# Another order of the same blocks: new tables for a hand-ordered attention and SwiGLU kernel

## The chip, the cores and the metric

The kernel runs on one core of one Trainium2 chip. A core has TensorE (matmuls, with weight loads shown on a row of their own), VectorE (DVE), ScalarE (ACT), GpSimd (POOL) and SyncE (SP), which here issues nearly all DMAs. Each engine works through its own instructions strictly in the order in which they were written, and waits where an input or a buffer is not ready. The metric is the device time of one execution in microseconds.

## The reference

For each of four batches, 32 inducing points attend to 12416 rows of x, which gives a small matrix h; then every row of x attends to h. The result goes through an RMS norm and a SwiGLU block with 1536 hidden columns, in FP32.

```python
def mab(q, kv):
    s = scale * (q @ kv.transpose(0, 2, 1))
    s = s - s.max(-1, keepdims=True)
    a = np.exp(s)
    a /= a.sum(-1, keepdims=True) + 1e-09
    return a @ kv
h = mab(I, x)                         # (4, 32, 128)
x = mab(x, h).reshape(B * S, D)       # (49664, 128)
...
rms = np.sqrt(np.mean(x * x, axis=-1, keepdims=True) + 1e-06)
xn = x / rms * rms_g
g = xn @ w_gate
silu = g * (1.0 / (1.0 + np.exp(-g)))
val = xn @ w_val
return (silu * val @ w_out).astype(np.float32)
```

## The kernel before

**Units and blocks.** A batch is cut into seven sets of rows (five of 2048, one of 1920, one of 256), and the first six sets into four quarters: 25 units of 512, 480 or 256 tokens each, 100 units over the batches. For each unit the twelve slices of 128 hidden columns are worked through one by one. A unit and a slice make a block; there are 1200.

**What a block does.** The second attention's weights, normalised so that the RMS norm is already in them, stand in a tile `a` as two rounded halves (`hi`, `lo`, each 32 rows, twice). The products of h with the gate and value weights stand as halves in `sg` and `sv`. So a gate is one matmul in the fast FP32 format, `gate` (L709), and a value one more, `value` (L737). ACT takes SiLU of the gate (`silu`, L719), DVE multiplies with the value (`times_value`, L751) and gives u. Then u is projected by the output weights `wo`, in one of three ways, the block's kind:

- P: `project_plain`, one plain FP32 matmul of u (L807, input `u,wo`).
- S: the product stays in PSUM; ACT makes a high half (L764), DVE the low half (L770), two matmuls project them (L795, L796) into one accumulator, POOL adds the halves in place (L815), and a third matmul projects the sum (L807, other inputs) into the other accumulator.
- D: as S, but u goes to SBUF, ACT makes the high half (L761), POOL the low one (L777), ACT scales the high one down (L783), and from the two matmuls on it is like S.

When a unit's blocks are done, `scale_up` (ACT, L839), `finish` (DVE, L848) and `turn_out` (DVE, L854) make its output, which `store` writes with four DMAs (L867). `gather` brings a unit's `a` together with four DMAs from the halves (L647); two such tiles are in turn.

**What runs beside.** While the blocks of one batch run, the attention of the next is prepared in small steps: loads of x by channels (`load_channels`, L111), DVE transposes of them (L299), scores (L316), exponentials, sums (L369), the output weights' halves, the norm (L548 to L608) and the split into halves (L627 to L635). There are 871 such steps, `micros`. At the start, weights are rounded on DVE, ACT and POOL (L204 to L260) and multiplied with h (`stack_of`, L485).

**What sets the order.** Nothing is scheduled when the kernel is built. One long string, `program`, is read letter by letter: `g` is a gate, `s` a SiLU, `v` a value, `m` the product, `h`, `l`, `n`, `e` the halves, `q` the two projection matmuls, `d` the addition, `r` the third matmul, `p` the plain projection, `E F T O` the end of a unit, `a` a gather, and a dot is the next of the `micros`, whose numbers stand in `taken`. Every engine gets its share of this sequence in this order. Further tables say which buffer each step takes: `banks` which of the eight PSUM banks, `holders` which of the nineteen tiles for u and its halves, `workers` and `outputs` which work and output tile; `sorts` gives the kind of each block, and `picks` which of the waiting blocks a letter takes. The loop that reads them (`do` maps letters to steps):

```python
for name in "".join(program.split()):
    made = len(nc.cur_bb.bb.instructions)
    step, args = micros[int(next(taken))] if name == "." else (do[name], ())
    step(*args)
```

Waits follow from data and buffers: a step that writes a bank or tile waits for the last reader of what stood in it.

Of the kernel before, what the change touches and what calls it, by code (L numbers as in the profile page):

```python
# [23 lines left out]
def kernel(  # L24
# [12 lines left out]
    m = inducing.shape[0]  # L37
# [1144 lines left out]
    def seams():  # L1182
# [13 lines left out]
        0234567021437052637152613076123067216073126071362016720162071620761270627410741203741231502137502137502153701530  # L1196
        7513074136507431570431672541765726152641756401725672543712453743143524750137502367261732107301627012670430123727
        2457321741357436527365202760327325036725032746326047312630140172403274015274312453714714671356717354107235410245
        1324135042130531073506735031756305617051253720372430520374053745236074537630431031706473061372461267514742764521
        7426543172632516730257156701350357064317064306247604062475027064571427015701537414213547231472513467541350463150  # L1200
        4135046530241564363016430176301746301724630716207516205321056310261405631574316371536741670456306751067102652057
        2570126507142571245714235174271354270643276345276527346275327464152364526345324502643056413206415027561207561057
        6120376253172142674561426541270564217045720437142741037126407236257342653475367264157637164314017360713604137607
        4153756345315215634160254310523104571230451204750416205421602364013503052413547032451724657142637162314761234712
        3467123061421325614532426756053075620562357230167501653176417534675671362457214235120321370157312510367250617564
        6246041712160421736230173616071561637601563075643764532645234256325143521463251305402503254234720472536420736027
        3464167462061270416071521050616521063215031025463152603176031635071736051630154702432124157134512745163721641206
        4236143613260413670326470260237052670325710263517253237543154713273561247623407636270612071023610256751467251462
        5176514725641357613615617036710536057167102571271470254724107521460152403514325431423014250145301504305450370457
        6302456730245632431206523026312560712037614261013071437201357240153425304614620136014620132014327345207354037540  # L1210
        2354673046215406215046510265402650264765072673250632753604327453715052054517420714756210425601352103210650263501
        7653145075065351375061750537215403140537120142307203142031643127532654512435625142305364502347052367327642576324
        7321437250437524375240732605413251427141346124361724173062413602410536140351406351436547065203405306524502340267
        3402640230634026413062167403641036401351463514056734256741265243124631623562041354163257435731516547635016741571
        2056215625460216452130420643274320436076204753264357614213471362376423016720472014564152420641205340263275602475
        2760574025176254637251372457143152307451204715276510761026517365023640576042734350423754210753702132370210726135
        2071362073462130143061402134561042615067156215427546172534526134063456145601634507645174607462071274126702671347
        0360135017673617536072361251725374327341534752362145362341301503520450137243031702310612067032613760521705620412
        7405170124073517354014607436746574053764052364721307063710726317503274052374062032764271603274026703653627620756
        735062731567235627  # L1220
    """
    workers = """
        2012012012012011021021120120120102201211210210201022012021021021
    """
    outputs = """
        10101010101010101010101010101010101010101010101010101010101010101010101010101010101010101010101010101010
    """
    holders = """
        abcdefghiabdcejkflmgnohibapqdrscefhgljibmkedpqnorscalhgfbmjiednkcgorfabdpsieqlmocgnpafrshkjdbqlimonregqlcspmoakj
        fhdqlbspnimrqkolesjgpncmraqdohfkiblsmpnojrqkmelnspgcjqaromsblhdfkpnjroicqmlgasnerkbplojqmfsdrhqnkaplmogbsrikjpql  # L1230
        ncmofesrkjdhpmlnaqogbcisrdkjlnepmhqkjolnpmfjosabrlnpcmjdoqgkhrlnpsoemjikrlnfqpbcsmjoldaqkspnmrjlqgoknhesicprfmlo
        qjnkspdormbgjeknqpslomjqrhaksonpfirlmjcqdobnrekpmshjqgloanikfrjpmslqndokrsbjlcpmeqohgnkraifpmsjbcelqhondgkrsjpml
        oqnikfcbpralsemjhgdoqcbkpenrlmsjfgoqkpalmisjnorkdqplmbhcnroqklefgsmpjaknilrdohqsbcmefpgadicjkafnliropqbsmjkcdnrp
        lfoqghasmeijkbncrpdfglohiqsjmebakngqsrpfjmdchiloegknfqsbrpkcajnqlsodrmpkqgiljhnsapbcdermokqnsplhaojkrqfgsnlmojkr
        dpqiblmcsnekroajslngmphqkorfdljcnqbkmspliornjqkemlsporangqhdfieskjmbciopaqldrnjmshrfnjqslgcbaokeprnqimljsdonkqph
        fcrmlobkqgnjaspedrmfhncigbjlokqsrmepnjlqsrmpnqodkscrmjlbqhokaspniefqrgmjlospkqdnclbosmhkanroqmpejsglkfonqrmlipch
        jsdoknqrmpjlboksrmnlapoegsqkjmrlposkqjmfnrlpoihkjcbaqlsmepndokgrjfsqhomrljkcpnisqoramljbekpsnfdqogrmhjlkpscqaieb
        jkglrpofsncqmhijkaedpoblsgrncqjfhmkpiabrnelmpgfqsjkordplmnqjahombckpnsirqefjlgkdpnahsormbckqejplnrsigfdkojqampcr
        lbesnhjqfkmiopdrlsnajqckmoprgbejlhsniqrokpmjsfdlacqneprmjgoshlbifcqnkmpjrodslagkqnmipjsherlckoqpfjnbmsrdkgaljqok
        pinmecrsfljhakpgqbinodcmrslqkjneposfalqhmkbgrjdcenspmokifrjalpqmohbnlgersipjkqomnfrcbpsdjkglohqmrnjpkeloasqbmrnj  # L1240
        pgcfklosinjmqahrpdecbgikladmqnofijrhbcspgklmqaednfoklspjrmnohqklpbicsjrqknmlorkpnsqgjmefoklrnpqhjdoabslikmcqjfrn
        pokqmgsjlrponmkqsjlrpondkslbhjmerpqnikasloqcnkjfghesldrnpomkqjsbcalpmokhqrsnjlikpemqdrfgcosnbkjamoilphqredgsnfbk
        jclpmoqrsnakjilpmoqrhsedfmnlobkpgcajqrslomnikphfloersdmnjqckprlsmojgbnqaifkpojhsrlmedcgnqsobaifhkjedglmcrpsnqklo
        bjmfrpeqsaknildgcjmoqhsknlbrfapoiqjrmskneplcoqjdrmskgnphljofqrbmsaknplojiqrcmeskodpjnmgblqfsrokpjnhsrmolkapqnjsi
        emroldkpqscnjoblkmpfrqhsnjompgerlkjoaqmspirndkljocbfhqmspkelgirnqmspajlkdohrcbfqnsjmoprgkeqlsnijmaporkqfslcbpnoj
        rmkshqdlrogmeijpqkclnsrabomfjpqhdiklgsnjqrpomsekncjlrabopfmqskdjhlonrgpmskqlijoncbprmskqeljnofpramsdkgqlhpicbenj
        mroskpqflmrosknjdpqhrgosaklmnpicqjbokesrflmpqnhsjdlraopmqkngscoljbmipksoqnedlrjmasoqfhpnkjmgcsloqprmnbiedkjsplra
        monkfqgjslprmcoqhnkjeslbipramnkoqjdgsfhlmpkocqnjrislaemopqjhnrdksbplfjmngkcioqsrpnljmkaeoshdqlfgrpicjnbae
    """
    sorts = """  # L1250
        PPPPPPPPPPPPPDDDPPPSPDPPDPPDPDPSSDPPDPDPPDPPPPPSDDDPDPDPSPSPSDPDSSPPPPSSPSSSSDSPSDPSSPDSSSSSSSDPSPSDDPSSPSPSDPSD
        SSDSSSSSPSDSPSSPPSSPSPDDPPDPSPSSPSDSSSDSPSDPSSPSSSPSDSSPPSDSPSSSSSSDPSSPDSSSSSSSPSSSSSSSSDSDPSSSSDPSSPSPSSSSSSSP
        PSDDDSPPSSPDPPSPPSDSSSSPDPSPDPDPSDPPSSPSPSSPDSSSPSPPSSPSPPSPSSPSPDSDPDPPPDPPSSDPSSDDDPDPPPSSDPDPSPPSPPSPSDDDPPPS
        PDPSPSDSSDSSSPDDPDPSSSSSPSSDSSSDDPPSPSSSSDPSSPSDPPSSSSSSDSSPSSSDPSPDPDSPSSSSSSSSDPSSSPSPSSSDDPSDPDPPSPPPSDSSSDSS
        SSSDPSSPSSDPSPDSSSSPSSSSSSSSDPSPSSDSPPSSSSSSSSSSSSSSSSSSDSSSPPDPSDSPSPDPSSSSPSPSSDSDPSPDSSPSSSSDSPSDPDPPPSPDSDPS
        PPSPDSDPSSSSPSSPPSDPSSPPPSSPSPPSSPPSSDSSDPSDDPSDPSPPSSDSPSSPSPSPSPSDSSDPSPSPSDDPPDSSSSDPPSSPSDSDSPPSSSDSSDDPSPPD
        SPSPPDSSSSPSDDDPPPDSSDPSPSSSDSPSSSSSDPSDSPSSSSDSSPSSDPSDDPPSPPSPSDPDDPPSPDPPSPSSSSSSDSPSSSSSSSSSPSDSSSSDSPSPSPSS
        SSSSSSSSSSSSDDSSPSSDSSPSDSSSSPPSSSSSSDSDPSSPPSDSDPDPPSPPPSSSSSDSPSSPPDSSPDPPSSSDDPSPSPSSPSSSPSPPPPSSSDPPPPSSDDPP
        PSPSDSSSDPSPDDPPSSDSSPPSSPSSSSSPSSSSPSPSSPSSDSPSSPSSSSPDSPSSSSSSPSSSDSSPSSPSSSSDPSSPPSSSSSDSDSPSPSSSPSSSDSSSPSPS
        SSSDSPSSPSSSDPSSSSPSSSSPSSDDPSPSSSSPSSSSSDSSPPSSSPSSSDSSPSSPSSSDSDPSPSSPSSSPSSSSSSSSDPSSPSSDSPSPSPSSSDSPSSSPSSSS  # L1260
        SSDPSPSSPSSSSDSSSPSPSSDSSPSSSSPSDSPDSPSSSSPSSSSSSPDPSSSPSSPDSSPSSSSSPSPDPDPDPPPP
    """
    picks = """
# [231 lines left out]
```

## Time and profile before

| | |
|---|---|
| median of three runs | 1481.76 us (1481.65 to 1482.52) |
| profiled execution | 1481.53 us |
| its span in the trace | 1479.7 us |
| granted TensorE clock | 0.999 |
| first gate product at | 47 us |
| DMA queue of SyncE | 114.55 MB, 39.8% of 16 engines' span |

The profile gives, for each engine, the time in which it is busy; records of neighbouring instructions overlap, so a sum over instructions exceeds the busy time. A row of a group shows the line in the kernel, the engine, the operation, what it writes and reads, the count, the busy time, the mean length of one in ns, and then how long the engine was idle just before such an instruction and what ended that.

### The profile page before, as it was taken

What the parts mean: (1) busy time and instruction counts of PE and PEld (TensorE: products, weight loads), DVE (VectorE), ACT (ScalarE), POOL (GpSimd) and SP (SyncE); (2) the same over time, 40 slices, a digit from 0 to 9 for tenths busy, and PEclk for the clock granted to TensorE, in tenths of its full rate; (3) what the DMA queues carried; (4) which work ended last, traced back from release to release, by engine and by line L of the source; (5) the groups of instructions that cost most, each with busy time, mean ns of one, the idle gap of its engine ahead of it and who ended that gap; (6) DMA issues with size and microseconds to landing.
All of it is one profiled execution on the core that took longest, in us unless ns stands there. A gap on an engine that the chain in (4) does not pass through costs nothing.

```text
span 1479.7 us, 26001 instructions
## 1 busy us (share of the span) xinstructions
PE 1467.6 (99%) x7286; PEld 1102.4 (74%) x7286; DVE 1420.0 (96%) x2469; ACT 1309.5 (88%) x2605; POOL 1378.8 (93%) x1204
## 2 busy tenths in 40 slices
PE   9999999999999999999999999999999999999998
PEld 6566777877777777787777777777778777787787
DVE  6999998999999999999999999899999999999997
ACT  5798889889988898988998988988998989899997
POOL 1499998999999999999999999999989999999998
PEclk9999999999999999999999999999999999999999
DMA  7694324448453231465656321264232122222122
GB/s 286 129 127 94 68 40 92 88 116 128 78 102 73 42 70 32 94 136 103 116 89 117 56 44 29 43 136 107 58 63 45 33 38 38 42 38 42 36 43 35
DMA packets 391712, 116.28 MB, mean 79 GB/s; under 512 B 365584, under 2 KB 370704, under 8 KB 389008
## 3 DMA queue, kind: packets, MB, share of 16 engines
q1 hardware_dynamic: 390976, 114.55, 39.8%
q8 instruction: 58, 0.95, 0.3%
q14 instruction: 86, 0.70, 0.2%
q10 hardware_dynamic: 592, 0.08, 0.0%
HBM read 53.95 MB, written 27.00 MB: 55 GB/s over the span
## 4 chain that ended last, share of the span: by engine, by line
PE 94%; DVE 2%; DMA 1%; issue 1%; ACT 1%; POOL 0%; SPq 0%; DVEq 0%; ACTq 0%; POOLq 0%
PE gv L807 31%; PE gv L709 17%; PE gv L737 17%; PE gv L795 12%; PE gv L796 12%; PE gv L316 3%; PE gv L369 1%; PE gv L908 1%; DMA xn<-in_x_dram 1%; DVE u L751 0%; PE gv L569 0%; DMA xT<-in_x_dram 0%; PE gv L463 0%; DVE o L239 0%; DVE we L248 0%
## 5 line engine op out<-in xcount | busy, mean ns | idle before, releaser
L719 ACT ACTIVATE silu<-gv 128x512 f32<-128x512 f32 (+2 forms) x1200 | 671.4, 592 | 74.4 <-PE gv L709 55.9
L815 POOL TENSOR_TENSOR xn<-xn,xn 128x512 fp32r<-128x512 f32 (+2 forms) x486 | 605.0, 1264 | 15.5 <-PE gv L796 14.0
L709 PE MATMUL gv<-a,sg 128*128 128x512 f32 (+2 forms) x1188 | 482.1, 431 | 0.6 <-DMA a<-lo 0.6
L737 PE MATMUL gv<-a,sv 128*128 128x512 f32 (+2 forms) x1188 | 449.4, 411 | 0.3 <-ACT silu L719 0.2
L751 DVE TENSOR_TENSOR gv<-silu,gv 128x512 f32<-128x512 f32 (+2 forms) x643 | 422.1, 676 | 10.2 <-PE gv L737 5.0
L764 ACT ACTIVATE xn<-gv 128x512 fp32r<-128x512 f32 (+1 forms) x629 | 370.0, 598 | 32.9 <-DVE gv L751 27.0
L751 DVE TENSOR_TENSOR u<-silu,gv 128x512 f32<-128x512 f32 (+2 forms) x557 | 354.5, 652 | 12.2 <-PE gv L737 5.3
L807 PE MATMUL gv<-u,wo 128*128 128x512 f32 (+2 forms) x724 | 353.5, 573 | 1.1 <-DVE u L751 1.0
L770 DVE SCALAR_TENSOR_TENSOR xn<-xn,gv 128x512 fp32r<-128x512 f32 (+1 forms) x516 | 337.4, 664 | 8.9 <-ACT xn L764 6.2
L709 PEld LDWEIGHTS gv<-a,sg 128*128 128x128 f32 x1188 | 223.3, 189 | 106.6 <-issue 32.4
L737 PEld LDWEIGHTS gv<-a,sv 128*128 128x128 f32 x1188 | 222.9, 189 | 86.9 <-issue 21.4
L815 POOL TENSOR_TENSOR xn<-xn 128x512 fp32r<-128x512 f32 (+1 forms) x204 | 255.3, 1257 | 7.0 <-PE gv L796 4.0
L777 POOL TENSOR_TENSOR xn<-u,xn 128x512 fp32r<-128x512 f32 (+2 forms) x174 | 218.2, 1260 | 15.7 <-ACT xn L761 15.2
L815 POOL TENSOR_TENSOR u<-xn,u 128x512 fp32r<-128x512 f32 (+2 forms) x133 | 167.9, 1271 | 2.1 <-PE gv L796 1.9
L795 PE MATMUL gv<-xn,xn 128*128 128x512 f32 (+1 forms) x441 | 169.7, 385 | 0.0
L807 PEld LDWEIGHTS gv<-u,wo 128*128 128x128 f32 x724 | 134.9, 190 | 27.9 <-issue 10.9
L795 PE MATMUL gv<-xn,more 128*128 128x512 f32 (+2 forms) x355 | 137.6, 388 | 0.0
L796 PE MATMUL gv<-xn,xn 128*128 128x512 f32 (+2 forms) x363 | 135.9, 374 | 0.0
L807 PE MATMUL gv<-xn,xn 128*128 128x512 f32 (+2 forms) x363 | 135.0, 383 | 0.5 <-POOL xn L815 0.3
L783 ACT ACTIVATE xn<-xn 128x512 fp32r<-128x512 f32 (+2 forms) x194 | 122.0, 633 | 10.8 <-POOL xn L777 9.2
L761 ACT ACTIVATE xn<-u 128x512 fp32r<-128x512 f32 (+2 forms) x194 | 121.0, 625 | 6.9 <-DVE u L751 6.1
L807 PE MATMUL gv<-xn,more 128*128 128x512 f32 (+2 forms) x311 | 118.8, 396 | 0.0
(223 smaller groups left out, 1787.8 us busy)
## 6 DMA issues: line engine op xcount, KB each, us to landing
out_dram<-o SPq DMA_DIRECT2D x320, 64.0 KB, 2.0
xT<-in_x_dram SPq DMA_DIRECT2D x60, 256.0 KB, 4.6
xn<-in_x_dram SPq DMA_DIRECT2D x60, 256.0 KB, 5.8
a<-hi SPq DMA_DIRECT2D x156, 64.0 KB, 2.0
a<-lo SPq DMA_DIRECT2D x156, 64.0 KB, 2.0
xn<-in_x_dram SPq DMA_DIRECT2D x5, 1024.0 KB, 9.6
xn<-w SPq DMA_DIRECT2D x18, 256.0 KB, 4.2
out_dram<-o SPq DMA_DIRECT2D x64, 60.0 KB, 2.0
```

The lines of the kernel that those rows point to most:

```text
L709: nc.tensor.matmul(g[:, 0:T], stacks[b][0][:, ts(j, P)], halves_in_turn(one["a"][:, 0:T]), start=True, stop=True)
L719: nc.scalar.activation(sl[:, 0:T], gates.pop(n)[:, 0:T], AF.Silu)
L737: nc.tensor.matmul(v[:, 0:T], stacks[b][1][:, ts(j, P)], halves_in_turn(one["a"][:, 0:T]), start=True, stop=True)
L751: nc.vector.tensor_tensor(out=to, in0=sl[:, 0:T], in1=v[:, 0:T], op=ALU.mult)
L764: nc.scalar.activation(hi, t["u"], AF.Copy, scale=-(1.0 - 2.0 ** -13) * 2.0 ** -12)
L770: nc.vector.scalar_tensor_tensor(out=t["lo"], in0=t["hi"].bitcast(F32), scalar=4096.0, in1=t["u"], op0=ALU.mult, op1=ALU.add)
L777: nc.gpsimd.tensor_tensor(out=t["lo"], in0=t["u"], in1=t["hi"].bitcast(F32), op=ALU.subtract)
L783: nc.scalar.activation(t["hi"], t["hi"].bitcast(F32), AF.Copy, scale=-(2.0 ** -12))
L795: nc.tensor.matmul(to, weight_of(0, j), halves_in_turn(t["hi"]), start=not one["q"], stop=False)
L796: nc.tensor.matmul(to, weight_of(1, j), halves_in_turn(t["lo"]), start=False, stop=last)
L807: nc.tensor.matmul(to.rearrange("p (n h) -> p h n", h=2) if step2 else to, lhsT, rhs, start=one["left"] == NJ, stop=one["left"] == 1)
L815: nc.gpsimd.tensor_tensor(out=t["lo"], in0=t["hi"].bitcast(F32), in1=t["lo"].bitcast(F32), op=ALU.add)
```

## The change

The eight tables `program`, `taken`, `banks`, `outputs`, `holders`, `workers`, `sorts` and `picks` have new contents; no function and no buffer changes, and neither does anything ahead of the first gate on TensorE. (`workers` and `outputs` are short, with 64 and 104 entries as before.) The new `program` has 10920 letters instead of 10915; `taken` names the same 871 steps in another order, most of it close to the old one. In `sorts`, P stands 358 times instead of 362, S 658 instead of 643 and D 184 instead of 195.

```diff
     banks = """
-        0234567021437052637152613076123067216073126071362016720162071620761270627410741203741231502137502137502153701530
+        0234567023147502635270132567123657315627316275312675321753215327512571632571624503125301543254132501543015430543
...
     workers = """
-        2012012012012011021021120120120102201211210210201022012021021021
+        2102102102102201021021210210210202102112120120102011022121021021
...
     sorts = """
-        PPPPPPPPPPPPPDDDPPPSPDPPDPPDPDPSSDPPDPDPPDPPPPPSDDDPDPDPSPSPSDPDSSPPPPSSPSSSSDSPSDPSSPDSSSSSSSDPSPSDDPSSPSPSDPSD
+        PPPPPPPPPPPPPPPPSPDPDPSPDDDPPPSPSPSPPDPDPPSDPPPSDDPDPDDPPPSPPSPSSSPSDPSSPPDSSDPSSPSSPDDSSDSPDPSSPPSSSDSSSSSDSSPS
...
     taken = """
-        9 1 0 5 10 80 6 2 7 54 41 81 13 3 45 106 108 46 4 11 17 55 42 18 47 43 107 19 25 12 21 26 14 56 29 20 15 105 59
+        1 0 5 54 9 80 2 6 79 41 3 10 81 4 42 17 13 7 18 106 43 107 11 25 12 19 45 108 21 55 20 46 44 8 26 14 56 105 22
...
```

The beginnings of the two sequences, dots with their numbers, show the kind of change (first gates, SiLUs, values, products and plain projections):

```
before  9 1 0 g 5 g 10 80 6 s s 2 g 7 g 54 41 s g 81 v v v 13 3 45 106 m 108 m 46 p s m 4 s g 11 v s
after   1 0 5 g g 54 g 9 80 s 2 s 6 79 g s 41 3 10 g 81 v v v m v 4 42 17 s 13 7 18 p 106 m 43 107 m s v p m
```

More of the change, by code (lines that the diff above doesn't have):

```diff
@@ L1200 @@
[L1200 to L1204, printed above, removed]
@@ new lines @@
+        5430571467051042014627461047614270642703460265346035631345104165340637416345617456724561451724650721543725305230
+        5132735012360123642106346013602143620135624015360213021703612031027126410745070725741704215704621740624061720710
+        4172307230647236472347524763257463250631740137503704157345713014356143643565136416325146320513605235062307253620
+        7305136576351764516375134761547316423172037601630172361023512571047303451353457031560457625472504256406247064256
+        7305436304653416534165034153642052030632705635726703156273162743526352143615243160540367543175107154031754013407
@@ new lines @@
+        1342716041304043716041426374263543564736247357436734504165304606143651307461354647316413672416471364120764231453
+        1736724172347631026124360456413651326342516325136216731247121342731207340731271540724072450762450642705642063726
+        5316310321352126017235013623564561263264135246175326715265237067526352760327560256123546256146315236540236401267
+        4320174031403127405214305230154025604125607421065465215326152364156241531120615205160526572160527165230572347120
+        3712347013402374235730576037526035706325602743262160240321401642132405640627060265742062750641706247601763026127
@@ new lines @@
+        6320513705610354131603416035401263402343641730643107634136075416034670142704327034130247104352102641345342164524
+        3716534653416540361543615403726107316053610736501765370614315764274314515612346152015304102410254725107425170517
+        4021174621637217427614302673407542762735230560536720562071025704251254123053150145213602436130121420134723140237
+        0254120417264127412754163542715267546257620674250725463072540372150720342017240723127602375253672032635273052617
+        0527156261264724572164731524713547307031274012734016273465706102170272467410673216425102510235610526130235067026
@@ new lines @@
+        SPSSDSPPSSSSSSSSDPSSDSPPSSSDSSPSSSSSPSSDSSDSDSPPSSPSSPSSSSSPPSSDDSDPPPPSPPSSDPSPSDPPSSSSSSSSSSSSSSSSSSPDPSSSPDPS
+        SSSSSSPSSDSSSSSSSSDSSDPSDSPSPDSPSPSSSSSSSSPDSDSDSPSPPPSPPSSSPSDDPSSPSPDPDPDPDPSPPSSPSSSDPSPSSSPPPSPSPSSPSSSDDPSP
+        SSPSDPDPDDSSPSSPSSPSSSSDPPSPPPSSSSSSSSSPSDSDSPSSPSSPSSSSSSSSDSPSPSSSSSSDSPPPSSSSSPSPDSPSSSSSSSDPSPSSSSSDSPSSSSDS
+        PPSSSSSDSPPSSSSSSDPSSPPSSSSSSSSSPSSPSDSDSPSSPSSPSDSSSSPDSPSSPSSSSDSPSSPSSSSSSDPSSPSPSSSSSSSSDSPSSSPSSSDDSPPSPPSS
+        SSSDPSSPSSPSSSSSSSPSSDSSPSSSDSPPSSSSSSSDPSSPPSSDSSSPSSPSSPSSDSSPSSSPSSSPSDPDPPPP
```

367 lines of the change are left out of this document (176 added, 191 removed), and 58 rows, old and new, of the table taken.

## The prediction

> **What bounds the kernel.** I read the page first: the busy shares, then the chain that ended last.
>
> ```profile
> span 1479.7 us, 26001 instructions
> ...
> PE 1467.6 (99%) x7286; PEld 1102.4 (74%) x7286; DVE 1420.0 (96%) x2469; ACT 1309.5 (88%) x2605; POOL 1378.8 (93%) x1204
> ...
> PE 94%; DVE 2%; DMA 1%; issue 1%; ACT 1%; POOL 0%; SPq 0%; DVEq 0%; ACTq 0%; POOLq 0%
> ```
>
> Four engines are nearly full, and the chain of waits is TensorE. Its busy share alone does not prove that it streams at its rate, because the records of successive matmuls overlap. So I looked at start times in its timeline (start, duration, both in us):
>
> ```profile
> 1000.02 1.02 PE L807 MATMUL gv<-u,wo 128*128 128x512 f32 x2
> 1000.48 0.78 PE L709 MATMUL gv<-a,sg 128*128 128x512 f32 x1
> 1001.10 0.38 PE L795 MATMUL gv<-xn,xn 128*128 128x512 f32 x1
> 1001.31 0.38 PE L796 MATMUL gv<-xn,xn 128*128 128x512 f32 x1
> 1001.53 0.38 PE L709 MATMUL gv<-a,sg 128*128 128x512 f32 x1
> ```
>
> Matmuls of 512 columns start 0.216 us apart (1001.10, 1001.31, 1001.53). I call that a pass. The plain FP32 projection (kind P, two records) and the gate behind it take 1001.10 - 1000.02 = 1.08 us, that is, five passes: four for P, one for the gate. Kinds S and D project with three passes (L795, L796, L807). So a P block costs one pass more than an S or D block. Narrower passes, from the same view:
>
> ```profile
> 1445.19 0.37 PE L796 MATMUL gv<-xn,xn 128*128 128x480 f32 x1
> 1445.39 0.37 PE L709 MATMUL gv<-a,sg 128*128 128x480 f32 x1
> ...
> 1471.18 0.28 PE L709 MATMUL gv<-a,sg 128*128 128x256 f32 x1
> 1471.29 0.28 PE L795 MATMUL gv<-xn,xn 128*128 128x256 f32 x1
> ```
>
> That is 0.20 us for 480 columns (0.2025 over a run of them) and 0.11 us for 256.
>
> Then the stages, in windows (length; busy time and count of PE, weight loads, DVE, ACT, POOL; granted clock, DMA share, GB/s):
>
> ```profile
> 40.00:80.00 40.00, 37.34 (x155) 20.98 (x156) 37.42 (x69) 32.16 (x64) 23.77 (x23) 1.00 0.63 120
> 80.00:120.00 40.00, 40.00 (x152) 25.33 (x151) 38.62 (x65) 36.73 (x71) 36.66 (x38) 1.00 0.92 133
> 120.00:160.00 40.00, 39.96 (x177) 28.05 (x176) 39.47 (x67) 36.34 (x75) 37.78 (x37) 1.00 0.35 69
> 160.00:200.00 40.00, 40.00 (x199) 28.81 (x197) 39.54 (x74) 33.96 (x67) 39.49 (x33) 1.00 0.34 68
> 1300.00:1400.00 100.00, 100.00 (x425) 78.83 (x425) 99.91 (x167) 92.45 (x177) 99.24 (x81) 1.00 0.21 39
> ```
>
> From 80 us on TensorE has no gap that the records show. What it loses lies in the stage from the first gate product on, and its groups there are (columns of the last part: busy us, mean ns, idle before):
>
> ```profile
> L807 PE MATMUL gv<-u,wo 128*128 128x512 f32 x26 | 13.3, 601 | 1.1 <-DVE u L751 1.0
> L709 PE MATMUL gv<-a,sg 128*128 128x512 f32 x18 | 9.9, 595 | 0.6 <-DMA a<-lo 0.6
> L737 PE MATMUL gv<-a,sv 128*128 128x512 f32 x17 | 7.2, 481 | 0.0
> L316 PE MATMUL gv<-xT,hT 128*32 128x512 f32 (+1 forms) x34 | 4.3, 588 | 0.0
> L485 PE MATMUL gv<-xn,hg 128*128 128x512 f32 x8 | 4.2, 610 | 0.1
> ...
> 46.98:76.70 29.72, 27.99 (x105) 13.60 (x105) 28.30 (x48) 23.70 (x46) 17.20 (x15) 1.00 0.74 146
> ```
>
> In passes this stage holds 18 gates, 17 values, 13 P projections (26 records) at four, four FP32 products of L485 at four, and four sets of L316 (eight records each, four column tiles at once) at four and one at two: 18 + 17 + 52 + 16 + 18 = 121 passes, 26.1 us of 29.72. So 3.6 us are lost; the rows name 1.0 us of waits for the product u and 0.6 us for the landing of the second unit's columns.
>
> The last matmul and the work behind it:
>
> ```profile
> 46.99 0.70 PE L709 MATMUL gv<-a,sg 128*128 128x512 f32 x2
> ...
> 1474.34 0.49 PE L807 MATMUL gv<-xn,more 128*128 128x256 f32 x2
> 1475.87 1.54 ACTq L867 DMA_DIRECT2D out_dram<-o  x2
> ```
>
> Between first gate and last matmul lie 1427.4 us. The gates, values and projections that the tables list make 5071 passes of 512 columns, 1026 of 480 and 265 of 256 columns: 1331.5 us. The attention's matmuls, the same in both kernels, I count in the same way at 80.2 us (an estimate). About 15.7 us are left: 3.6 in the first 30 us, 12 in the other 1398. Part of the 12 is what small matmuls cost beyond passes. I take 4 us of it as waits, an estimate, since the rows above run without a gap. The whole room for a better order is thus some 7 us.
>
> **The change part by part.** Startup ahead of the first gate and the work behind the last matmul (4.9 us) keep their instructions; I cost both at nothing.
>
> *Block kinds.* P goes from 362 to 358, S from 643 to 658, D from 195 to 184. By width, P changes by -4 at 512 columns, +6 at 480, -6 at 256; S by +18, -9, +6; D by -14, +3, 0. On TensorE: -4 x 0.216 + 6 x 0.2025 - 6 x 0.11 = -0.3 us. That is all that the path itself loses. The other engines:
>
> ```profile
> L764 ACT ACTIVATE xn<-gv 128x512 fp32r<-128x512 f32 (+1 forms) x629 | 370.0, 598 | 32.9 <-DVE gv L751 27.0 <-PE gv L709 0.5 <-PE gv L807 0.4
> L770 DVE SCALAR_TENSOR_TENSOR xn<-xn,gv 128x512 fp32r<-128x512 f32 (+1 forms) x516 | 337.4, 664 | 8.9 <-ACT xn L764 6.2 <-ACT rt L594 0.4 <-POOL xn L815 0.4
> L783 ACT ACTIVATE xn<-xn 128x512 fp32r<-128x512 f32 (+2 forms) x194 | 122.0, 633 | 10.8 <-POOL xn L777 9.2 <-POOL u L777 0.9
> L761 ACT ACTIVATE xn<-u 128x512 fp32r<-128x512 f32 (+2 forms) x194 | 121.0, 625 | 6.9 <-DVE u L751 6.1 <-issue 0.2
> L719 ACT ACT_TABLE_LOAD x13 | 16.7, 1283 | 0.5 <-PE gv L709 0.3
> ...
> 51.42 1.88 DVE L751 TENSOR_TENSOR u<-silu,gv 128x512 f32<-128x512 f32 x3
> 53.98 0.67 DVE L751 TENSOR_TENSOR u<-silu,gv 128x512 f32<-128x512 f32 x1
> 1002.33 1.10 ACT L719 ACTIVATE silu<-gv 128x512 f32<-128x512 f32 x2
> 1002.34 3.77 POOL L815 TENSOR_TENSOR xn<-xn,xn 128x512 fp32r<-128x512 f32 x3
> ```
>
> Back to back, an instruction of 512 columns takes (1.88 - 0.67) / 2 = 0.60 us on DVE, 1.10 - 0.60 = 0.50 on ACT (the mean of L764 taken off; L761 and L783, 0.03 longer, 0.53) and 3.77 / 3 = 1.26 on POOL; the means in the group rows are longer because neighbours overlap. In units of 512 columns, S changes by 18 - 8.4 + 3 = +12.6, D by -14 + 2.8 = -11.2, S and D together by +1.4. So DVE gains 12.6 x 0.60 = +7.6 us (L770). ACT gains 12.6 x 0.50 = 6.3 (L764), loses 11.2 x 2 x 0.53 = 11.9 (L761, L783) and, by the instruction lists, two of its table loads, 2 x 1.283 = 2.6: -8.2 us. POOL loses 11.2 x 1.26 = 14.1 (L777) and gains 1.4 x 1.26 = 1.8 (L815): -12.3 us. ACT and POOL lie beside TensorE and their relief costs and gives nothing by itself. DVE's 7.6 us fit into its 59.7 us of idle time, if they come where it idles; that is the case against the change.
>
> *Where DVE's work goes.* I counted both instruction lists from the first value and its product to block 200. Before, DVE has 242.7 us to do while TensorE has 249.1; after, 249.4 against 249.7 (ten more L770 and one L248). So nearly all of the 7.6 us falls into the first 200 blocks. From block 300 on the lists agree within 1 us per 300 blocks.
>
> *The first 30 us.* The first product stands one DVE instruction earlier (an L248 is now behind it), and four values instead of three precede the first P; that covers the first wait for u. Against it, DVE has nine instructions more and one less ahead of the 25th product (four L299, two L548 among them): 35.5 against 31.1 us, where TensorE has 33.1 against 32.1, so DVE ends 2.4 us behind and has caught up by block 48. Between the value of block 0 and the projection of block 40, DVE needs 0.6 us more than TensorE's own work offers, so at least that is a wait. Bounds: -1.6 us (all named waits gone) and +2.4 (the lag is exposed whole). The 0.6 us for the landing stay: that gate is again the fifth and the gathers are issued in the same order. I take -1.0, nearer the named waits, because eight PSUM banks let TensorE go on.
>
> *Order, banks, buffers behind that.* The distance from a value to the projection that needs its halves, counted in TensorE time, is least 2.0 us before and 2.3 after for S (median 4.9 and 5.0); value to P has medians 5.3 and 5.2; from the first two projection matmuls to the third 4.3 and 3.9, above one POOL instruction of 1.26. The engine chains between them are as long as before, so the slack is about the same, a little more where ACT and POOL work.
>
> *DMAs and queues.* SyncE issues as many transfers as before; the loads of the next batch are moved past output stores and gathers. The tightest gather is that of the fifth unit:
>
> ```profile
> 113.27 1.28 SPq L647 DMA_DIRECT2D a<-hi  x1
> ...
> 115.86 0.58 SPq L647 DMA_DIRECT2D a<-lo  x1
> ...
> a<-lo SPq DMA_DIRECT2D x156, 64.0 KB, 2.0
> ```
>
> Issue to landing is 116.4 - 113.3 + 2.0 = 5.2 us. TensorE work between this gather's place and the unit's first gate is 5.4 us before, 6.7 after; all others have over 6.3 before, 7.6 after. Since the gather ahead of it SyncE issues two shifts more and one load less than before; that could delay it by one issue, 0.6 us, which the extra 1.3 covers. I cost the queue at nothing; uncovered, it is that 0.6.
>
> For everything from block 48 on: bounds -4 us (all waits gone) and +6.7 (all of DVE's extra exposed). I take -0.9, about a quarter of the waits, since the order's slack is so nearly the same.
>
> Sum: -0.3 - 1.0 - 0.9 = -2.2 us. The profiled execution took 1481.53 us (span 1479.7 and 1.8 around it), which gives 1479.3; the median of the runs is 0.2 higher, so **1479.5 us**. One can tell 0.2% from no change here, that is 3.0 us: the forecast is "within".
>
> **The rivals.** *More of the waits go.* If early and late waits fall by 3.5 to 7 us, the time is about 1476.5. For it speak the looser ACT, POOL and gathers; against it that nothing on the TensorE side changes and DVE is tighter.
>
> *DVE becomes the bound in the first 200 blocks (slower).* From 40 to 200 us it was busy 37.42 + 38.62 + 39.47 + 39.54 = 155.05 of 160 us, 96.9%. At that share its 249.4 us take 257.4. Before, TensorE passed these blocks in 249.1 + 3.6 + some 0.9 lost = 253.6. So +3.8 us: 1485.5; with a worse share up to 1487. It decides from where DVE cannot reach 249.4 / 253.6 = 98.3%. The window 1300 to 1400 shows 99.91% with TensorE full, so it can; but there no startup work is mixed in.
>
> *DVE is the bound throughout (slower).* If TensorE's passes hid real idle time and DVE at 96% set the pace, its 7.6 us would all be on the path: 1489.3. Against it stand the even steps of 0.216 us. The Trainium skill (Perfetto Trace Analysis, section Identifying the Most-Contended Engine) says that matmul busy share is no measure for TensorE, that the share of weight loads is, and that occupancy is fair for VectorE; by that rule, with 74% against 96%, VectorE would be the engine to watch and the change a loss. The trace disagrees here: FP32 projections run four passes on two weight loads, which thins the loads without any gap between the passes.
>
> *Nothing net.* The waits move elsewhere: 1481.8, give or take 1.
>
> **How the numbers follow.** Forecast 0.42 (its own range 1478 to 1482), more waits gone 0.22, early DVE bound 0.24, DVE bound throughout 0.04, nothing net 0.08. Faster by over 0.2% (under 1478.8): all of the second and 0.12 of the first, 0.34. Slower by over 0.2%: 0.24 + 0.04 = 0.28. Within: 0.38. The range 1475.0 to 1487.0 leaves out the tail of the second case (0.05), the worst of the DVE case (0.05) and the DVE bound throughout.
>
> **What would show it.** Right: steps of 0.216 us as before; in the 30 us behind the first gate fewer than 3 us lost and less than 1 us named for u; DVE at 98.3% or more between 48 us and block 200 with TensorE without gaps. Wrong: TensorE rows with idle time released by DVE (L751, L770) in the first 250 us; a gate of the fifth unit waiting for a<-lo; a DVE busy share there under 98% while TensorE's lost time exceeds 4.5 us.

## The result, and the profile after

The changed kernel takes 1478.32 us (median of nine runs, 1476.76 to 1479.58). The ratio to the kernel before is 0.9977, with a 95% interval of 0.9967 to 0.9987: 3.4 us, or 0.23%, faster. The forecast was 1479.5 us. Its own bound for "faster" was 3.0 us, so the outcome that it held likeliest ("within") was missed by 0.4 us, on the side of the first rival.

The page of the kernel after, in the lines that were shown of before (span; busy time; chain of waits):

```profile
span 1476.3 us, 26012 instructions
...
PE 1464.3 (99%) x7290; PEld 1102.3 (75%) x7290; DVE 1428.1 (97%) x2484; ACT 1302.0 (88%) x2596; POOL 1366.7 (93%) x1197
...
PE 95%; DVE 2%; ACT 1%; DMA 0%; issue 0%; POOL 0%; SPq 0%; DVEq 0%; POOLq 0%; ACTq 0%
```

DVE has 8.1 us more work, ACT 7.5 us less, POOL 12.1 us less. The span falls by 3.4 us all the same. DVE's idle time (span less busy) goes from 59.7 to 48.2 us: 11.5 us less, which is the 8.1 us of new work and the 3.4 us of shorter span. That is the first thing to see: in the new order DVE stands idle less. It is not yet a reason for the shorter span.

The windows of after (length; busy time and count of PE, weight loads, DVE, ACT, POOL; granted clock, DMA share, GB/s):

```profile
40.00:80.00 40.00, 38.25 (x147) 21.69 (x147) 38.27 (x69) 31.29 (x63) 22.72 (x23) 1.00 0.68 124
80.00:120.00 40.00, 40.00 (x186) 24.66 (x185) 39.22 (x66) 35.82 (x69) 33.19 (x33) 1.00 0.70 114
120.00:160.00 40.00, 40.00 (x159) 29.48 (x158) 39.49 (x68) 36.71 (x77) 38.17 (x36) 1.00 0.59 109
160.00:200.00 40.00, 40.00 (x200) 29.15 (x199) 39.92 (x75) 33.51 (x65) 39.90 (x34) 1.00 0.23 42
48.00:300.00 252.00, 251.13 (x1233) 177.80 (x1226) 248.24 (x425) 221.72 (x432) 224.83 (x198) 1.00 0.50 93
```

The last row reaches to about block 200, whose gate starts at 303 us. DVE is busy for 98.5% of it. Before, the same window was:

```profile
48.00:300.00 252.00, 250.23 (x1211) 174.76 (x1206) 241.99 (x411) 225.86 (x437) 228.52 (x201) 1.00 0.50 92
```

That is 96.0%. What DVE waited for, from 48 to 255 us (total, times, longest), before:

```profile
DVE xn L770 <- ACT xn L764: 2.0, 3, 1.4
DVE u L751 <- PE gv L737: 1.6, 3, 1.0
DVE gv L751 <- ACT silu L719: 1.2, 3, 0.6
DVE u L751 <- ACT xn L761: 1.1, 1, 1.1
```

and after, the whole list:

```profile
DVE e L354 <- ACT sc L347: 0.7, 1, 0.7
DVE o L848 <- ACT o L839: 0.7, 1, 0.7
DVE u L751 <- ACT silu L719: 0.4, 2, 0.2
DVE u L751 <- ACT xn L764: 0.2, 1, 0.2
DVE u L751 <- PE gv L737: 0.2, 1, 0.2
DVE gv L751 <- ACT silu L719: 0.2, 1, 0.2
DVE xn L770 <- ACT xn L764: 0.2, 1, 0.2
```

Waits for ACT's halves and for values have all but gone. From 48 to 1475 us DVE's waits for a value, before and then after:

```profile
DVE u L751 <- PE gv L737: 5.3, 13, 1.0
DVE gv L751 <- PE gv L737: 5.0, 15, 0.8
```

```profile
DVE u L751 <- PE gv L737: 1.7, 7, 0.4
DVE gv L751 <- PE gv L737: 1.0, 4, 0.3
```

That is 7.6 us less, close to the 8.1 us that DVE has more to do, but the two do not stand in the same place. Ahead of 300 us, where DVE has 6.2 us more to do (241.99 and 248.24), the waits for values fall by 1.8 us and those for ACT by 3.3. The other 5.8 us of waits for values go behind 300 us, where DVE's work grows by only some 2 us.

TensorE's side. I take its loss at a block's gate as the time since the first gate less the passes ahead of it, counted as in the prediction. At the gates of blocks 48, 200, 480, 600 and 1199 (119, 304, 638, 781 and 1471 us in the trace of before) the loss was 4.4, 7.4, 9.8, 10.8 and 15.8 us before; it is 2.7, 5.0, 6.8, 10.0 and 12.6 us after. The new order gains 1.7 us by block 48, 3.0 us by block 480, gives 2.1 us back between blocks 480 and 600, and gains that back by the end. Nearly half of what it gives back is one wait. TensorE's timeline of after, with the idle time and its releaser in brackets:

```profile
778.49 0.28 PE L796 MATMUL gv<-xn,more 128*128 128x256 f32 x1
779.71 0.45 PE L709 MATMUL gv<-a,sg 128*128 128x512 f32 x1 [0.94 <-DMA a<-lo]
```

This is the first gate of unit 50, the first of the third batch. SyncE's queue ahead of it:

```profile
772.14 3.46 SPq L867 DMA_DIRECT2D out_dram<-o  x4
775.71 0.54 SPq L647 DMA_DIRECT2D a<-hi  x1
```

POOL's last low half for that batch's first set was ready at 771.99 us, and DVE's transpose for the store at 770.28 us:

```profile
770.72 1.27 POOL L635 TENSOR_TENSOR lo<-aT,hi 128x512 fp32r<-128x512 f32 x1
769.62 0.66 DVE L854 STREAM_TRANSPOSE o<-o 128x480 f32<-128x480 f32 x1
```

The data for the gather were there at 772 us, but an output store stands ahead of it and holds the queue until 775.6 us. Its four writes take 3.46 us to issue; the transpose was done before the first of them started, and what else made them slow is not shown.

### The profile page after: what moved, and what is told of

Read it like the earlier page. It is cut to its first block, busy times and chain, and to the rows that moved or that the text cites. A ratio compares the mean times of both kernels' runs of the same rounds, so it can differ in the third digit from the quotient of the medians.

```text
span 1476.3 us, 26012 instructions
## 1 busy us (share of the span) xinstructions
PE 1464.3 (99%) x7290; PEld 1102.3 (75%) x7290; DVE 1428.1 (97%) x2484; ACT 1302.0 (88%) x2596; POOL 1366.7 (93%) x1197
## 4 chain that ended last, share of the span: by engine, by line
PE 95%; DVE 2%; ACT 1%; DMA 0%; issue 0%; POOL 0%; SPq 0%; DVEq 0%; POOLq 0%; ACTq 0%
PE gv L807 31%; PE gv L709 17%; PE gv L737 17%; PE gv L795 12%; PE gv L796 12%; PE gv L316 3%; PE gv L369 1%; PE gv L908 1%; DVE u L751 1%; PE gv L569 1%; PE gv L463 0%; PE gv L152 0%; DMA a<-lo 0%; POOL xn L815 0%; SPq L647 0%
## 5 line engine op out<-in xcount | busy, mean ns | idle before, releaser
L815 POOL TENSOR_TENSOR xn<-xn,xn 128x512 fp32r<-128x512 f32 (+2 forms) x467 | 579.1, 1256 | 22.4 <-PE gv L796 17.2
L751 DVE TENSOR_TENSOR gv<-silu,gv 128x512 f32<-128x512 f32 (+2 forms) x658 | 431.4, 674 | 4.7 <-ACT silu L719 1.9
L764 ACT ACTIVATE xn<-gv 128x512 fp32r<-128x512 f32 (+2 forms) x633 | 371.0, 597 | 36.2 <-DVE gv L751 27.7
L751 DVE TENSOR_TENSOR u<-silu,gv 128x512 f32<-128x512 f32 (+2 forms) x542 | 345.4, 655 | 8.2 <-ACT silu L719 3.9
L807 PE MATMUL gv<-u,wo 128*128 128x512 f32 (+2 forms) x716 | 353.0, 577 | 0.1
L770 DVE SCALAR_TENSOR_TENSOR xn<-xn,gv 128x512 fp32r<-128x512 f32 (+2 forms) x520 | 339.6, 664 | 5.5 <-ACT xn L764 3.4
L815 POOL TENSOR_TENSOR xn<-xn 128x512 fp32r<-128x512 f32 (+2 forms) x216 | 268.8, 1252 | 9.1 <-PE gv L796 7.7
L777 POOL TENSOR_TENSOR xn<-u,xn 128x512 fp32r<-128x512 f32 (+2 forms) x163 | 202.1, 1245 | 13.6 <-ACT xn L761 9.2
L795 PE MATMUL gv<-xn,xn 128*128 128x512 f32 (+2 forms) x430 | 163.5, 380 | 0.0
L807 PEld LDWEIGHTS gv<-u,wo 128*128 128x128 f32 x716 | 133.3, 190 | 28.3 <-issue 10.4
L807 PE MATMUL gv<-xn,xn 128*128 128x512 f32 (+2 forms) x366 | 141.1, 393 | 0.0
L796 PE MATMUL gv<-xn,xn 128*128 128x512 f32 (+2 forms) x366 | 136.5, 373 | 0.0
L761 ACT ACTIVATE xn<-u 128x512 fp32r<-128x512 f32 (+2 forms) x180 | 111.9, 623 | 8.5 <-DVE u L751 7.7
L783 ACT ACTIVATE xn<-xn 128x512 fp32r<-128x512 f32 (+2 forms) x180 | 113.0, 632 | 3.3 <-POOL xn L777 2.7
L807 PE MATMUL gv<-xn,more 128*128 128x512 f32 (+2 forms) x304 | 115.5, 390 | 0.0
```

What stands on the lines that cost most here:

```text
L751: nc.vector.tensor_tensor(out=to, in0=sl[:, 0:T], in1=v[:, 0:T], op=ALU.mult)
L764: nc.scalar.activation(hi, t["u"], AF.Copy, scale=-(1.0 - 2.0 ** -13) * 2.0 ** -12)
L770: nc.vector.scalar_tensor_tensor(out=t["lo"], in0=t["hi"].bitcast(F32), scalar=4096.0, in1=t["u"], op0=ALU.mult, op1=ALU.add)
L777: nc.gpsimd.tensor_tensor(out=t["lo"], in0=t["u"], in1=t["hi"].bitcast(F32), op=ALU.subtract)
L783: nc.scalar.activation(t["hi"], t["hi"].bitcast(F32), AF.Copy, scale=-(2.0 ** -12))
L795: nc.tensor.matmul(to, weight_of(0, j), halves_in_turn(t["hi"]), start=not one["q"], stop=False)
```

## The experiments

A splice below is one sequence up to the gate of some block, and from there the steps of the other sequence that are not yet done, in its order. Steps that the other sequence had already done by that gate come first, in a burst. The kernel before took 1481.3, 1481.2 and 1481.0 us in the three jobs.

### The gather ahead of the store

`program`, with the dots' numbers, at the place in question:

```diff
-q m O g 777 m p h l s g l v r s 427 d v q v m g E q m p d s a 440 h g
+q m g 777 a O m p h l s g l v r s 427 d v q v m g E q m p d s 440 h g
```

> The changed kernel with one gather moved: that of unit 50 (the first of the third batch) now stands right behind the POOL step that makes its last low half and ahead of the output store that stood before it on SyncE's queue. Theory A (the store ahead of it, which waits for DVE, is what made TensorE wait 0.94 us for a<-lo at 780 us): the four transfers start at about 772 instead of 775.7 us, the wait of 0.94 us is gone, and the time falls from 1478.3 to about 1477.4 us. Rival (the other engines use that wait to catch up, so TensorE pays it at a later place): the wait for a<-lo is gone but the time stays at 1478.3 us, give or take 0.4.

Measured: 1476.02 us (1475.89 to 1476.51), ratio to before 0.9965 (0.9951 to 0.9978). SyncE's queue and the same gate:

```profile
771.06 0.66 SPq L647 DMA_DIRECT2D a<-hi  x1
...
773.83 2.17 SPq L867 DMA_DIRECT2D out_dram<-o  x4
```

```profile
777.50 0.28 PE L796 MATMUL gv<-xn,more 128*128 128x256 f32 x1
777.61 0.38 PE L709 MATMUL gv<-a,sg 128*128 128x512 f32 x1
```

The gate follows the matmul ahead of it after one narrow pass, 0.11 us. Theory A holds, the rival falls: the time does not come back. The gain is 1.9 us (5.3 under before, where the changed kernel is 3.4 under it), more than the 0.94 us expected. Between the two profiled runs the step at this gate is 1.1 us; the other 0.8 us fell ahead of 745 us (some 0.6 of it between 693 and 704 us), where the two kernels have the same instructions, so I put it down to scatter between executions. That fits the run with other tiles below, which keeps the late gather and a wait of 0.7 us for it: it is 4.1 us under before, 1.0 to 1.2 us behind this one. So the gather's place is worth some 1.1 us, close to what was expected. The five runs lie within 0.6 us, those of the changed kernel within 2.8. This version is the fastest of all here; its interval still overlaps that of the changed kernel.

### Splices with new buffers

```diff
-program: before's letters
+program: after's letters up to the gate of block 119 (e2) or 487 (e3), then before's;
+         before's up to 487, then after's (e4)
-banks, holders, workers: as written
+the one free longest, counted in steps
```

> The changed kernel's sequence and kinds up to the gate of block 119 (some 150 us of TensorE work), behind it the sequence and kinds of the kernel before; banks, work and u tiles are all given out anew, always the one that has been free longest. Theory A (the gain is waits that the new order avoids, and each stage's gain stands by itself): the loss curve falls by 1.7 us up to the cut and then runs beside that of the kernel before, so about 1480.1 us. Rival B (the gain is the tables of banks and buffers, not the order): the three spliced kernels of this job, which share one rule for buffers, come out equal. Rival C (DVE paces the kernel): the ten extra low halves fall into this part, so it is slower than before, 1485 us.

> As the kernel spliced at block 119, but with the cut at the gate of block 487 (some 590 us of TensorE work). Theory A: the gain up to there is 2.8 us, and the order of the kernel before avoids the stretch from 650 to 780 us where the changed kernel gives 1.5 us back, so about 1479.0 us, with the loss curve of the kernel before, shifted, behind the cut. Rival B: equal to the other two spliced kernels. Rival (splicing costs waits of its own): a step in the loss curve at the cut.

> The other way round: the sequence and kinds of the kernel before up to the gate of block 487, those of the changed kernel behind it, buffers by the same rule as in the other two spliced kernels. Theory A: of the 3.1 us that the two loss curves differ by at the end only 0.3 come from behind this cut, so about 1481.4 us. Rival B: equal to the other two, some 1478 to 1479 us.

Measured: 1483.77, 1483.80 and 1482.02 us, ratios 1.0016 (1.0007 to 1.0025), 1.0017 (1.0008 to 1.0026) and 1.0003 (0.9994 to 1.0011). Theory A's numbers for e2 and e3 (1480.1, 1479.0) are missed by 3.7 and 4.8 us; that for e4 (1481.4) lies within its interval. Rival B has two of the three equal, but not the third and not at its 1478 to 1479 us, and Rival C comes within 1.2 us for e2. These runs cannot choose, because two things were mixed in them. Up to its cut, e3 runs the changed kernel's instructions in the changed order, with other buffers, and yet it is 2.1 us behind it at 381 us, most of it in steps of some 0.4, 0.7 and 0.4 us at 87, 360 and 381 us; and e2 loses 2.8 us within 31 blocks behind its cut, where the kernel before loses 1.2. The next four runs take the two apart.

### Each part with its own tables

```diff
-mixture cut at 119 or 487, buffers by one rule
+after up to the gate of block 150, then before (e5); before up to 694, then after (e6);
+each part keeps its banks and buffers
```

> The changed kernel's sequence and kinds up to the gate of block 150, behind it those of the kernel before; this time each part keeps its own tables of banks and buffers (the names in the second part are exchanged once at the cut, so that what is in use there keeps its place). Theory A (the new order avoids waits, stage by stage): the loss up to this cut is 2.5 us lower, and from there the curve runs beside that of the kernel before, so 2.5 to 2.8 us less than it: about 1478.8 us where the kernel before takes 1481.4. Rival C (DVE paces the kernel, the gain lies elsewhere): no gain or a loss. Theory D (what cost the first spliced kernel its gain was the choice of the bank that had been free longest in the sequence): no step at the cut and no new waits for SiLU.

> The other way round: the kernel before up to the gate of block 694, the changed kernel behind it, each with its own tables. This leaves out the changed kernel's store and gather at 770 to 780 us. Theory A: behind this block the changed kernel loses 2.8 us and the kernel before 4.9, so 2.1 us less: about 1479.3 us where the kernel before takes 1481.4. Rival (all of the gain lies in the first 150 blocks, and what the curves differ by later is chance): the same as the kernel before, within 0.5 us.

Measured: 1480.56 us, ratio 0.9995 (0.9986 to 1.0004), and 1483.79 us, 1.0017 (1.0008 to 1.0026). In e5 the loss is the changed kernel's up to just ahead of the cut, 2.3 us under before; behind it TensorE waits:

```profile
243.76 0.48 PE L737 MATMUL gv<-a,sv 128*128 128x512 f32 x1 [0.85 <-ACT silu L719]
```

At 252 us 0.7 us of lead are left, at the end 0.35, so Theory A's 1478.8 us is missed. Theory D also expected no step at the cut: that is wrong. In e6 TensorE loses 2.6 us within eight blocks of its cut, where the kernel before loses nothing, with these waits among them:

```profile
894.51 0.70 PE L807 MATMUL gv<-xn,xn 128*128 128x512 f32 x2 [1.36 <-POOL xn L815]
901.14 0.48 PE L795 MATMUL gv<-xn,xn 128*128 128x512 f32 x1 [0.77 <-ACT xn L783]
```

and never makes it good: neither Theory A's 1479.3 us nor its rival's 1481 holds. So with the written buffers a splice still costs 1.5 to 3 us at the seam.

### Banks or tiles

```diff
 banks = """
-        0234567023147502635270132567123657315627316275312675321753215327512571632571624503125301543254132501543015430543
+        0234567023147502635270132567123657315627316275312675321753215327521572631572641503245302513451234502513025130513
```

```diff
 holders = """
-        abcdefghiabcdfeghjkialmbdnopqcfrsgjkehnoibdlmpqcfarsgheijkcnlafpmrobdsqighrojneclpfkmabdgsqrohijeclpksmnfbqraokg
+        abcdefghiabcdfeghjkialmbdnopqcfrsgejhikbdcfnlopagimqhedarsijkgcnolmbfqpahedicgbflrhmjeabfnksohdqpaiefcblhgmrdnjf
```

> The changed kernel with one table other: each step takes the PSUM bank that has been free longest as counted in steps of the sequence; order, kinds, u tiles, work and output tiles stay. Theory D (a bank that is freed by a SiLU behind a table load of 1.28 us comes free late in time, though early in the sequence; the written table knows this, the rule does not): the gates or values behind table loads wait for SiLU at 87, 360 and 381 us as they did in the kernel spliced at block 487, 2.0 us by 390 us, and the time grows by 3 to 5 us, to about 1482 us. Rival (it was the u tiles): same time as the changed kernel, about 1478.3 us.

> The changed kernel with one table other: each step takes the tile for u or a half that has been free longest; banks and all else stay. Theory D (the banks cost it): same time as the changed kernel, 1478.3 us within 0.7. Rival (it was the u tiles): slower by 3 to 5 us.

Measured: 1478.83 us with other banks, 0.9984 (0.9975 to 0.9992), and 1477.15 us with other tiles, 0.9972 (0.9960 to 0.9983). The tiles make no difference that stands clear of the intervals. The banks do what Theory D says, at its places: against the changed kernel TensorE is 0.4 us behind at 87 us, 2.0 at 360, 2.4 at 381 and 2.7 at 611. TensorE and ACT of the kernel with other banks, at the second of these:

```profile
361.54 0.47 PE L795 MATMUL gv<-xn,xn 128*128 128x480 f32 x1 [0.67 <-ACT silu L719]
```

```profile
355.85 1.28 ACT L451 ACT_TABLE_LOAD   x1
357.14 2.00 ACT L451 ACTIVATE sc<-sc 128x1024 f32<-128x1024 f32 x2
359.06 0.55 ACT L764 ACTIVATE xn<-gv 128x480 fp32r<-128x480 f32 x1
359.62 1.28 ACT L719 ACT_TABLE_LOAD   x1
360.92 1.50 ACT L719 ACTIVATE silu<-gv 128x480 f32<-128x480 f32 x3
```

ACT does the next batch's exponentials and loads its table for SiLU again. The gate's bank, counted as free because its SiLU stands earlier in the sequence, is still full in time, and the first projection into it waits. But the whole costs only some 1 us (0.9984 against 0.9977, with intervals that overlap), not 3 to 5. Because TensorE is still 2.0 us later just ahead of the gate of unit 50, its gather now comes in time: the list of waits has only one for a<-lo, 0.5 us, that of the start. One loss hides another.

### A cut where the sequences are closest

The letters around the cut of e9 (to the left of the bar is what stands ahead of the gate of block 80):

```diff
-g d q l s v r s F p h 633 m v | g m h v g n T s q g
+g v e 184 r q 632 d q s F 633 m v | g m h v g n T s q g
```

> The changed kernel's sequence, kinds and tables up to the gate of block 80 (some 104 us of TensorE work), those of the kernel before behind it. The two sequences stand closest there (one load of rows, one transpose and a few steps of the last blocks apart), and no table load of ACT is near. Theory A (the gain of the first stage stands by itself): the loss at the cut is 1.5 us lower and stays so; with one P block more than the kernel before (0.2 us) it takes 1.3 us less than it. Theory E (an order is worth its gain only together with what follows: another order behind it finds ACT, POOL and DVE elsewhere and waits): the lead of 1.5 us is given back at the next load of ACT's tables (105 or 220 us), and the time is that of the kernel before, within 0.5 us, or above it.

> The kernel before up to the gate of block 79, behind it the changed kernel with the gather of unit 50 moved ahead of the store (which alone took 1476.0 us where the kernel before took 1481.3), each part with its tables. Theory A: it loses the first stage's 1.5 us and, by its kinds, gains 0.2: about 1477.4 us where the kernel before takes 1481.3. Theory E: waits behind the cut take more than that, 1479 us or above.

Measured: 1480.92 us, 0.9999 (0.9990 to 1.0008), and 1479.56 us, 0.9990 (0.9981 to 0.9998). The first is Theory E's number, but not its place: the lead of 1.5 us at the cut is gone six blocks later, before any table load of ACT. The timelines of e9, first DVE, then TensorE:

```profile
159.64 0.69 DVE L770 SCALAR_TENSOR_TENSOR xn<-xn,gv 128x512 fp32r<-128x512 f32 x1 [0.66 <-POOL xn L815]
```

```profile
160.82 0.48 PE L737 MATMUL gv<-a,sv 128*128 128x512 f32 x1 [0.61 <-ACT silu L719]
```

I read it so: TensorE had its lead at that gate, but ACT, DVE and POOL had not. The burst shows what they owed to before's sequence: a transpose (184), F and m on DVE, 632 and a SiLU on ACT, 633 and d on POOL. The second run is 2.2 us above Theory A's 1477.4 and in Theory E's range. Theory A, that each stage's gain stands by itself, finds no support: no cut kept its whole lead. Each cut has such a burst of its own, though, so these runs do not tell a lead that was never real from one that the seam destroyed.

### 7.2 us more on DVE

```diff
-            nc.vector.tensor_tensor(out=to, in0=sl[:, 0:T], in1=v[:, 0:T], op=ALU.mult)
+            for _ in range(2 if n in (50, 52, 54, 57, 66, 69, 77, 85, 101, 135, 138, 144) else 1):
+                nc.vector.tensor_tensor(out=to, in0=sl[:, 0:T], in1=v[:, 0:T], op=ALU.mult)
```

> The kernel before with DVE's product done twice in 12 blocks of kinds P and D between blocks 50 and 144; the second writes the same tile with the same values. 12 x 0.60 = 7.2 us more on DVE and nothing else. Theory F (TensorE is the bound and DVE has some slack in the first 200 blocks; from 40 to 200 us it was idle for 4.9 us): it costs 2.2 us or more, less than 7.2: about 3 to 5 us, 1485 us. Rival C (DVE paces the kernel): all of it, 7.2 us, 1488.5 us. Rival (DVE's extra is hidden as the changed kernel's 8 us were): under 1 us, 1482 us.

> The changed kernel with the same 12 products done twice, 7.2 us more on DVE. In it DVE was idle for 3.1 us from 40 to 200 us. Theory F: 4.1 us or more, up to 7.2, so more than the same addition costs the kernel before: about 5 to 7 us, 1484 us, with TensorE waiting for DVE (u, the low halves) between 100 and 250 us. Rival C: 7.2 us, 1485.5 us, the same as in the kernel before. Rival (hidden): under 1 us, 1479 us.

Measured: in the kernel before 1487.81 us, 1.0046 (1.0034 to 1.0059), 6.8 us more; in the changed kernel 1483.70 us, 1.0018 (1.0009 to 1.0026), about 6 us more (6.1 by the ratios, 5.7 between the profiled spans). Waits of TensorE from 100 to 260 us, before and after with the extra work (the edit makes L751 L752):

```profile
PE gv L709 <- DVE u L752: 1.1, 2, 0.8
PE gv L737 <- DVE u L752: 0.8, 2, 0.5
PE gv L808 <- DVE u L752: 0.6, 1, 0.6
```

```profile
PE gv L737 <- DVE u L752: 1.5, 3, 0.6
PE gv L709 <- DVE u L752: 0.6, 2, 0.3
```

The loss curves say where the extra work is paid. In the kernel before, the first nine products (blocks 50 to 101) cost 5.1 of their 5.4 us, the last three (blocks 135 to 144, at 231 to 240 us) only 1.0 of 1.8; another 0.4 us stands ahead of the first of them and cannot come from them. The last three lie in a window in which DVE had 5.5 us of idle time:

```profile
200.00:255.00 55.00, 55.00 (x278) 40.66 (x278) 49.47 (x82) 53.31 (x99) 49.23 (x41) 1.00 0.36 73
```

The changed kernel has 53.25 us of DVE work in the same window:

```profile
200.00:255.00 55.00, 55.00 (x284) 41.94 (x283) 53.25 (x89) 52.08 (x101) 49.44 (x41) 1.00 0.39 78
```

Here the first nine products cost 5.3 us and the last three 2.0: by block 155 all of the 7.2 us is paid. Behind 704 us the difference is 0.8 us smaller. But the profiled run of the changed kernel, which I compare with, itself lost some 0.6 us between 693 and 704 us that the run with the moved gather did not lose either, so most of this is the scatter met there. So the kernel before fits Rival C's 7.2 us better than Theory F's 3 to 5, and the changed kernel, though its time is in Theory F's range, pays like Rival C in this stretch. Extra work in DVE's products there is paid nearly in full, except where DVE stood idle. That the changed kernel's own 8 us were free fits this, since its order fills such idle time (10.0 us of 252 before, 3.8 after, in the windows to 300 us), but no run moved that work alone.

## Why the prediction was right or wrong

*TensorE is the bound, and the room is some 7 us.* The steps stayed at 0.216 us (starts at 1000.01, 1000.22 and 1000.44 us in the timeline of after), the chain of waits at 95% TensorE. But TensorE is not alone: between blocks 50 and 144 DVE is nearly as tight, as the doubled products show. Of the 7 us, some 3 are gained by the changed kernel and some 5 by the one with the moved gather (loss at the last matmul 15.8, 12.8 and 10.8 us).

That the sum came within 1.2 us of the time is in part luck. The gather's wait, put at nothing, cost some 1.1 us, and the other waits gave way by more than the forecast took for them.

*Block kinds, -0.3 us.* Right: the passes between first gate and last matmul come to 1411.6 us before and 1411.3 after. The work of the other engines was right to a microsecond (DVE +7.6 foreseen, +8.1 measured; ACT -8.2, -7.5; POOL -12.3, -12.1), and the tail stayed as it was (5.2 and 5.3 us of span from the start of the last matmul).

*The first 30 us, -1.0 us.* Right in sign and nearly in size. By the 129 passes in this group list of after (L807 and L485 four for two records, L316 four for eight), TensorE loses 3.05 us of 30.89 against 3.6 of 29.72:

```profile
L807 PE MATMUL gv<-u,wo 128*128 128x512 f32 x32 | 16.4, 605 | 0.1
L709 PE MATMUL gv<-a,sg 128*128 128x512 f32 x21 | 10.1, 530 | 0.7 <-DMA a<-lo 0.6 <-DVE sg L492 0.2
L737 PE MATMUL gv<-a,sv 128*128 128x512 f32 x20 | 9.0, 506 | 0.0
L485 PE MATMUL gv<-xn,hg 128*128 128x512 f32 x8 | 4.1, 592 | 0.0
L316 PE MATMUL gv<-xT,hT 128*32 128x512 f32 x16 | 2.1, 605 | 0.0
```

The wait for u is gone, as said, and 0.2 us for DVE's L492 has come instead. The mark set for "right" (under 3 us lost) is missed by a hair. By block 48 the gain is 1.7 us: the lag of DVE that was feared as +2.4 was not exposed.

*All from block 48 on, -0.9 us.* Right in sign, too small: before lost 15.8 - 4.4 = 11.4 us there, the changed kernel 12.6 - 2.7 = 9.9, so -1.5; with the gather moved it is 10.6 - 2.7 = 7.9, so -3.5. The weak step is "since the order's slack is so nearly the same". I measured slack on TensorE's clock, from a value to its projection, and that measure cannot see how seldom DVE stands idle, which did change. That TensorE's gain comes from it is not shown: between the gates of blocks 150 and 200 DVE's idle time falls from 1.7 to 0.3 us, and TensorE loses 1.2 us there before and 1.3 after.

*DMAs and queues, nothing.* This step was wrong. I took the place of each gather in the sequence and counted the TensorE work from there to the gate: over 7.6 us for unit 50. But SyncE's queue works in order, and the store just ahead held it for 3.46 us. The transfers started 3.7 us after their data were ready, the gate waited 0.94 us, and with the gather ahead of the store the time was 1.9 us lower (1.1 of it at this place). The expectation named DVE as what the store waits for; the transpose was done 1.9 us before the store's first write, so that part is not borne out. The gather named as the tightest, the fifth unit's, never waited.

*DVE becomes the bound in the first 200 blocks.* The rival named the right engine and the right limit: in the runs with doubled products 6 to 6.8 of the 7.2 us of further DVE work there are paid. Its failing step is the fixed share: it let DVE stay at 96.9% from 40 to 200 us. The share is a property of the order. It became 98.1% there (156.9 of 160 us, the sum of four rows above) and 98.5% to block 200, just above the 98.3% named as the point that decides.

*DVE is the bound throughout.* It did not happen: 8.1 us more DVE work and a shorter span. The Trainium skill (Perfetto Trace Analysis, section Identifying the Most-Contended Engine) would have one optimise the engine of highest occupancy, with weight loads, 75% here, as TensorE's measure. Its pick of VectorE is half borne out: between blocks 50 and 144 added DVE work costs nearly its full length, though in the changed kernel TensorE streams there without recorded gaps (40.00 of 40 us busy in three windows from 80 to 200 us). As a forecast of this change it fails, since it takes no account of DVE's waits giving way.

*More of the waits go.* This came nearest in mechanism: 3 us less loss in the changed kernel, 5 with the gather moved, against its 3.5 to 7. That nothing on the TensorE side changes was no argument against it.

*Nothing net.* Its 1481.8 us, give or take 1, is missed by more than 2 us.

What stays open: which of the many moves in the order bring the gain. Every splice changes the seam too, so the runs show only that no stretch kept its whole lead behind a cut. The cause of the changed kernel's 3.4 us is thus located (1.7 us by block 48, the rest in small pieces behind) but, apart from the moved gather, not isolated by a run.

## What to carry to other kernels

Where two engines are nearly full, add up the idle time of the second one, by what it waited for and by place, before and after: here new work on it was paid nearly in full where it had no idle time, and in part where it had. Do not count on grafting a stretch of one tuned order onto another: none of the cuts here kept the whole lead, and a lead on one engine can be a debt on three others. For every transfer that something waits for, look at what stands ahead of it in its issuing queue and how long that holds the queue, not only at how early it is written.

## What the runs showed of the hardware

A buffer's age in steps is not its age in time. Each change of ACT's table between exponentials and SiLU takes 1.28 us, and with the exponentials between two changes ACT is away from SiLU for 5 us (355.8 to 360.9 us in the rows above); a PSUM bank given out by steps alone was met full behind such a place three times in the first 390 us. The Trainium skill (ScalarE: Activation LUTs, section What ACT_TABLE_LOAD costs) gives 1283 ns for the load, as here, and another 1380 ns of drain for every switch. No such drain shows here: the load at 359.62 us starts when the instruction ahead of it ends (359.06 + 0.55), and the SiLU follows at 360.92.

Runs of one kernel scatter by different amounts: nine with the late gather lie within 2.8 us, five with the early one within 0.6. The late gather is not shown to be the reason, since six runs with other tiles, which keep it, lie within 1.0.
